# Sparse attention followed by a gated layer: where batch 1's attention sits inside batch 0's output products, and how batch 1's hidden layer begins

## The chip, the cores and the metric

The kernel runs on one core of a Trainium2 chip. That core has four compute engines, each with its own in-order stream of instructions: TensorE (PE in the profile; its weight loads are listed apart as PEld), VectorE (DVE), ScalarE (ACT) and GpSimd (POOL). A fifth stream, SyncE (SP), only issues DMA transfers; ACT and POOL issue some too. Streams wait for one another by semaphores, so an instruction that waits holds up everything behind it on its own engine.

The metric is the device time of one execution in microseconds (us). The kernel before was run three times: 217.37, 216.25 and 216.25, median 216.25.

## The reference, cut to what matters

Two stages. Attention over 4 batches, 8 heads, 768 positions and 64 channels a head: each query sees the keys less than 16 positions away, and one summary for each of the 24 blocks of 32 positions (largest key value per channel, mean of the values). Then a gated hidden layer over the 3072 rows of 512 channels.

```python
B, H, S, D = q.shape                       # 4, 8, 768, 64
block, window = (32, 16)
k_sum = k.reshape(B, H, nb, block, D).max(axis=3)
v_sum = v.reshape(B, H, nb, block, D).mean(axis=3)
scores_l = scale * np.matmul(q, k.transpose(0, 1, 3, 2))
mask_l = np.abs(pos[:, None] - pos[None, :]) < window
scores_s = scale * np.einsum('bhsd,bhnd->bhsn', q, k_sum) + np.log(block)
...                                        # softmax over both parts together
attn = np.matmul(a, np.concatenate([v, v_sum], axis=2))
x = attn.transpose(0, 2, 1, 3).reshape(B * S, H * D)
h = x @ w_in                               # 3072x512 by 512x2048
g = h * (1.0 / (1.0 + np.exp(-beta * h)))
out = g @ w_out                            # 3072x2048 by 2048x512
```

## The kernel before, in words

**Tiling.** Heads go in four pairs (g = 0..3), because two heads of 64 channels fill the 128 partitions. Batch by batch, three things are made:

- the attention output of the batch, laid down transposed in `xT` (four tiles of 128 channels by 768 rows; tile g comes from head pair g);
- the hidden layer `h_sb` (16 tiles of 128 hidden channels by 768 rows): for each tile, two halves of 384 rows, each a sum of four products over the four tiles of `xT` (L509), then one SiLU on ACT over both halves (L522);
- the output, six blocks of 128 rows, each a sum of 16 products of 128x512 (L527), copied from PSUM to SBUF and sent off by SP (L533). The sixteen products of a block are cut into four "atoms" of four, so there are 24 atoms in a batch.

**Staging.** The loops are software pipelined. While PE does the 24 output atoms of batch b, the attention of batch b+1 is put between the atoms; while it does the hidden layer of b+1, the inputs of batch b+2 are loaded, cast and transposed. The stage this study is about is the output of batch 0 with the attention of batch 1 in it, and the start of batch 1's hidden layer behind it.

**The order.** It is written out by hand. `run(main, sides)` walks through the main list (atoms 0 to 23), and after atom i gives out every side step whose position is below i + 1, in order of position. Each engine gets its instructions in the order in which the program gives them out. So a step at position 8.0 comes after atom 8, and its matmuls come before those of atom 9 on PE; the other engines' parts come in that order on their own streams.

**The steps of batch 1's attention**, for a head pair g and a half u of the rows:

- `load_v` (L103, L104) brings the values to `vst`; POOL casts them to `ve` (`v_cast`, L344); SP then moves rows of `ve` to `vo`, the copy shifted by half a tile, with two DMAs for each pair (`v_odd_dma`, L355 and L356). These are the "row moves" below.
- `km_pe` makes the largest key of each block on DVE (L233) and copies it beside the key windows on POOL (`key_sums`, L241).
- `scores` are 12 small matmuls (L328) into one of three PSUM buffers `big`, then an Exp on ACT (L335) and a multiplication by the band mask on DVE (`mask_e`, L339).
- `vm_all` makes the block means of the values for all four pairs, 28 matmuls (L388) into the PSUM buffer `one[1]`, and four DVE casts out of it; it needs all four `v_cast`s. `spread` writes these means into rows 96 to 127 of `vo` and `ve` on DVE (L399). Since the row moves read those rows of `ve`, the second half of `spread` (pairs 2 and 3) waits for the row moves of pairs 2 and 3.
- AV are 24 matmuls for each pair (L414) into `big`, then a reciprocal (L440) and a multiplication (L441) on DVE into `xn` (together "norm"). `x_dma` transposes `xn` into `xT[:, g]` by a DMA that ACT issues (L466).
- `key_load` (L97) brings the keys of the batch after next; it only shares SP's stream and the DMA engines with the steps above.

**Buffers.** `one` has two PSUM banks: atoms of an even output block use `one[0]`, of an odd one `one[1]`. `big` has three buffers of two banks, used in turn by scores, AV and the hidden tiles (tile i in `big[i % 3]`).

**Start of the hidden layer.** `h_tile(0)` does three quarters of tiles 0 and 1 (the products with pairs 0, 1 and 2) before the last quarter of tile 0, which needs pair 3. Inside `h_part` the order is half by half, so the third matmul of all already needs pair 2.

Of the kernel before, what the change touches and what calls it, by code (L numbers as in the profile page):

```python
# [11 lines left out]
def kernel(  # L12
# [10 lines left out]
    nc = tc.nc  # L23
# [27 lines left out]
    k1 = d_model // P  # L51
    k2 = d_ff // P
# [13 lines left out]
    one = [ps.tile([P, 1, 512], f32, name=f"one{i}") for i in range(2)]  # L66
# [3 lines left out]
    def pair(a, b, g):  # L70
        return a[b, 2 * g:2 * g + 2]
# [22 lines left out]
    def key_load(b, g):  # L94
        f = stage.tile([RK, 2, CK * D], f32, name="kst", tag="kst")
        stg[("k", b, g)] = f
        nc.sync.dma_start(out=f[:], in_=pair(k, b, g).rearrange("h (p c) d -> p h (c d)", c=CK))  # L97
# [186 lines left out]
    def km_pe(g, ks):  # L284
        key_max_win(g)
        key_sums(ks, g)
# [97 lines left out]
    def vm_all(t, cps):  # L384
        M = P - NK
        for j in range(J6 + 1):
            for g in range(G):
                nc.tensor.matmul(t[g * M:(g + 1) * M, 0, 0:2 * D], A[:, j],  # L388
                                 strided(ve[:, g, j, 0:1], [[J6 * VW, 2], [1, D]]),
                                 start=(j == 0), stop=(j == J6))  # L390
        for g in range(G):
            cps[g](vm_sb[NK:P, :, g], t[g * M:(g + 1) * M, 0, 0:2 * D].rearrange("p (h d) -> p h d", h=2))

    def spread(gg):
        r = slice(NK, P)
        s = slice(2 * gg, 2 * gg + 2)
        for tt in (vo, ve):
            for h in range(2):
                nc.vector.tensor_copy(out=tt[r, s, h * J6:(h + 1) * J6, 0:D],  # L399
                                      in_=vm_sb[r, h, s, None, :].to_broadcast([P - NK, 2, J6, D]))  # L400
# [64 lines left out]
    def x_dma(b, g):  # L465
        nc.scalar.dma_start_transpose(out=xT[:, g, :].rearrange("p (j t) -> p j t", j=J6),  # L466
                                    in_=xn[(b, g)].rearrange("p j h d -> p (j h d)"))
# [37 lines left out]
    def h_part(i, k_lo, k_hi):  # L505
        t = big[i % 3]
        for kk in range(2):
            for ki in range(k_lo, k_hi):
                nc.tensor.matmul(t[:, kk, 0:HS], w_in_sb[:, ki, i * P:(i + 1) * P],  # L509
                                 xT[:, ki, kk * HS:(kk + 1) * HS], start=(ki == 0), stop=(ki == k1 - 1))  # L510

    def h_tile(i):
        t = big[i % 3]
        if i > 1:
            h_part(i, 0, k1)
        elif i == 0:
            h_part(0, 0, k1 - 1)
            h_part(1, 0, k1 - 1)
            h_part(0, k1 - 1, k1)
        else:  # L520
            h_part(1, k1 - 1, k1)
        nc.scalar.activation(out=h_sb[:, i, :].rearrange("p (k m) -> p k m", k=2), in_=t[:, :, 0:HS],  # L522
                             func=ACTF.Silu, scale=beta_sb[:, i:i + 1])

# [27 lines left out]
    def run(main, sides):  # L552
        sides = sorted(sides, key=lambda x: x[0])
        for i, f in enumerate(main):
            f()
            while sides and sides[0][0] < i + 1:
                sides.pop(0)[1]()
        for _, f in sides:
            f()
# [83 lines left out]
    s = []  # L643
# [32 lines left out]
    s = [(6, lambda: scale4(1)), (12, lambda: scale4(2)), (.5, clear_kw), (14, lambda: km_pe(0, nc.gpsimd))]  # L676
# [4 lines left out]
    def av_at(b, s, pos, bufs):  # L681
        for g in range(G):
            def av(g=g):
                for u in range(2):
                    av_mm(b, g, u, big[bufs[g]][:, u])
                norm(b, g, big[bufs[g]], [0, 1])
                if g == 0 and b > 1:
                    for u in range(2):
                        last_mask[b] = mask_e(b, G - 1, u)
            s.append((pos[g], av))  # L690

    def x_pe2(b, g, t):
        t = t.bitcast(bf16)[:, 0, 0:S]
        x = xn[(b, g)]
        for j in range(J6):
# [1 line left out]
        act_cp(xT[:, g, :], t)  # L697

    s = [(.05, exp_table), (.15, lambda: scale4(3)), (.2, lambda: km_pe(1, nc.gpsimd)),
         (.3, lambda: km_pe(2, nc.gpsimd)), (3.44, lambda: km_pe(3, nc.gpsimd))]  # L700
    main = [lambda ms=ms, a=a: o_atom(0, ms, a) for ms in range(J6) for a in range(4)]
    s.append((2.5, lambda: qt1([act_cp, dve_cp])))
    for g in range(G):
        s.append(((2.88, 2.89, 3.4, 3.5)[g], lambda g=g: v_cast(nc.gpsimd, g)))
        s.append(((2.885, 2.895, 3.45, 3.55)[g], lambda g=g: v_odd_dma(g)))
    for j, (g, u, bg, pos, late) in enumerate([(0, 0, 2, 4.5, 4.6), (0, 1, 1, 4.5, 4.61), (1, 0, 0, 4.5, 4.62), (1, 1, 2, 8, 8.2),
                                               (2, 0, 1, 8, 8.21), (2, 1, 0, 8, 8.22), (3, 0, 2, 11, 11.13), (3, 1, 1, 11, 11.14)]):
        s.append((pos + .01 * j, lambda g=g, u=u, bg=bg: scores(1, g, u, bg)))
        s.append((late, lambda g=g, u=u: last_mask.update({1: mask_e(1, g, u)})))
    s.append((11.09, silu_table))  # L710
    s.append((8.0, lambda: vm_all(one[1], [dve_cp] * 4)))
    s.append((8.1, lambda: spread(0)))
    s.append((8.11, lambda: spread(1)))
    av_at(1, s, [11.12, 15.1, 15.2, 15.3], [0, 1, 2, 0])
    for g in range(G):
        s.append(((11.2, 15.35, 15.4, 15.5)[g], lambda g=g: x_dma(1, g)))
    for g in range(G):
        s.append(((2.896, 2.897, 3.56, 3.561)[g], lambda g=g: key_load(2, g)))
    run(main, s)


# [3 lines left out]
    for b in range(1, B):  # L725
        n = b + 1
        s = []
        if n < B:
            for g in range(2):
                s.append((0 + .1 * g, lambda g=g, n=n: hw_load("q", q, n, g)))  # L730
            for g in range(G):
                s.append((.5 + g, lambda g=g: key_cast(n, g)))
                s.append((.6 + g, lambda g=g: kq_dma("k", n, g)))
                s.append((3.5 + g, lambda g=g: windows_perm(dve_cp, g, kT[g][:, 0:S].rearrange("p (c r) -> p c r", c=CK), CK)))
                s.append((3.6 + g, lambda g=g: key_max_win(g)))
                s.append((4.7 + g, lambda g=g: kq_cast(nc.gpsimd, "q", n, g)))
                s.append((8 + g, lambda g=g: key_sums(nc.gpsimd, g)))
                s.append((6.6 + 1.5 * g, lambda g=g: kq_dma("q", n, g)))
                s.append((12.6 + 1.2 * g, lambda g=g: v_cast(nc.gpsimd, g)))
                s.append((12.7 + 1.2 * g, lambda g=g: v_odd_dma(g)))  # L740
            for g in range(2):
                s.append((.7 + g, lambda g=g, n=n: hw_load("q", q, n, g + 2)))
                s.append((2.7 + g, lambda g=g: load_v(n, g)))
                s.append((6.7 + 1.5 * g, lambda g=g: load_v(n, g + 2)))
        if n + 1 < B:
            for g in range(G):
                s.append(((16.31, 16.32, 19.3, 19.31)[g], lambda g=g, n=n: key_load(n + 1, g)))
        late = [x for x in s if x[0] >= 16]
        run([lambda i=i: h_tile(i) for i in range(k2)], [x for x in s if x[0] < 16])
        s = [((x[0] - 16) * 1.2, x[1]) for x in late]  # L750
        if n < B:
            for j, (g, u, bg, pos, late) in enumerate(UNITS):
                s.append((pos + .01 * j, lambda n=n, g=g, u=u, bg=bg: scores(n, g, u, bg)))
                if g < G - 1:
                    s.append((late, lambda n=n, g=g, u=u: mask_e(n, g, u)))
            s.append((.05, exp_table))
            s.append((11.19, silu_table))
            av_at(n, s, [11.2, 14.1, 14.2, 14.3], [0, 1, 2, 0])
            for g in range(G):
                s.append(((11.3, 14.35, 14.4, 14.5)[g], lambda g=g: x_dma(n, g)))  # L760
            s.append((5.89, lambda: vm_all(one[0], [dve_cp] * 4)))
            s.append((8.3, lambda: spread(0)))
            s.append((8.31, lambda: spread(1)))
        main = [lambda ms=ms, a=a: o_atom(b, ms, a) for ms in range(J6 - (n == B)) for a in range(4)]
        run(main, s)
        if n == B:
            ms = J6 - 1
            for lo, hi in ((0, 256), (256, 512)):
                t = one[0 if lo else 1][:, 0]
                for kk in range(k2):  # L770
                    o_mm(ms, kk, t, lo, hi)
                o = op.tile([P, hi - lo], f32, name="o_half", tag=f"o_half{lo}", bufs=1)
                nc.vector.tensor_copy(out=o[:], in_=t[:, 0:hi - lo])
                nc.sync.dma_start(out=out_r[b * J6 + ms][:, lo:hi], in_=o[:])
# [29 lines left out]
```

## Time and profile before

| | |
|---|---|
| median of the three runs | 216.25 us |
| the profiled execution | 216.76 us |
| its span (first to last instruction) | 214.9 us |
| PE busy | 205.3 us, 96% of the span |
| DVE busy | 111.0 us |
| ACT busy | 106.8 us |
| POOL busy | 54.6 us |
| hidden products L509 (batches 1 to 3) | 384 matmuls, 63.1 us |
| output products L527 | 83.4 us |
| granted TensorE clock | 0.998 of full speed |

The page's busy times are shares of the whole span. Where something starts and what it waited for is read from the timeline and from the chain that ended last; times in those are microseconds from the first instruction. In this execution batch 0's output atoms start at 48.40 us and batch 1's hidden layer at 77.37 us.

### The profile page before, as it was taken

To read this page: it belongs to the slowest core of one execution; us is meant where nothing else is said; L and a number is where in the kernel's file an instruction comes from. 1 tells how busy PE (TensorE), PEld (TensorE's weight loads), DVE (VectorE), ACT (ScalarE), POOL (GpSimd) and SP (SyncE) were. 2 spreads that over 40 slices of the span, in tenths; PEclk is the share of its full clock that TensorE was granted. 3 is DMA by queue.
4 is the path that set the end of the run, shared out by engine and by line. 5 is a ranking of instruction groups with operands and counts; after the bars stand their busy time and mean duration, and the time that the engine had idled before them with its cause. 6 is when DMAs were issued, how large, how long until landed. Compare 5 with 4: busy or idle time off the path is not lost.

```text
span 214.9 us, 5279 instructions
## 1 busy us (share of the span) xinstructions
PE 205.3 (96%) x2221; PEld 121.7 (57%) x2238; DVE 111.0 (52%) x252; ACT 106.8 (50%) x141; POOL 54.6 (25%) x85
## 2 busy tenths in 40 slices
PE   7999999999988999999999999999999999999993
PEld 7777766655454456665555466654555566654452
DVE  5587785398657721970898325654787200002121
ACT  2458786686655107778633046777450076650000
POOL 7938990003610303553103004443000000000000
PEclk9999999999999999999999999999999999999999
DMA  6999999999998999999689979999535500001212
GB/s 125 185 214 183 186 171 203 207 205 179 190 261 241 165 162 238 226 200 159 152 230 276 192 169 230 154 212 195 141 119 108 151 18 0 0 3 49 98 49 98
DMA packets 74534, 34.08 MB, mean 159 GB/s; under 512 B 61440, under 2 KB 70032, under 8 KB 74512
## 3 DMA queue, kind: packets, MB, share of 16 engines
q1 hardware_dynamic: 57440, 24.05, 53.2%
q0 software_dynamic: 7440, 7.34, 21.4%
q10 hardware_dynamic: 9632, 2.37, 8.0%
q8 instruction: 17, 0.28, 0.5%
q14 instruction: 5, 0.04, 0.1%
HBM read 27.37 MB, written 6.29 MB: 157 GB/s over the span
## 4 chain that ended last, share of the span: by engine, by line
PE 64%; DMA 15%; POOL 7%; DVE 6%; SPq 4%; issue 3%; ACT 0%; POOLq 0%; DVEq 0%
PE big L509 29%; PE one L527 29%; DMA w_out_sb<-in_moe_w_out_dram 8%; DMA xT<-xn 2%; DMA vst<-in_v_dram 2%; PE one L544 2%; DMA vo<-ve 2%; PE big L328 2%; PE big L414 2%; DVE xn L441 1%; SPq L356 1%; POOL ve L344 1%; POOL vo L351 1%; POOL vo L352 1%; DVE e L339 1%
## 5 line engine op out<-in xcount | busy, mean ns | idle before, releaser
L527 PE MATMUL one<-w_out_sb,h_sb 128*128 128x512 bf16 (+1 forms) x383 | 83.4, 370 | 1.9 <-issue 1.4
L522 ACT ACTIVATE h_sb<-big,beta_sb 128x768 bf16<-128x768 f32 x48 | 42.7, 900 | 47.1 <-PE big L509 47.1
L509 PE MATMUL big<-xT,w_in_sb 128*128 128x384 bf16 x384 | 63.1, 326 | 0.1
L527 PEld LDWEIGHTS <-h_sb 128*128 128x128 bf16 x400 | 38.1, 98 | 41.3 <-issue 0.2
L509 PEld LDWEIGHTS <-w_in_sb 128*128 128x128 bf16 x384 | 37.6, 98 | 25.5 <-issue 0.4
L247 DVE COPY o_sb<-one 128x512 f32<-128x512 f32 x19 | 13.1, 690 | 45.8 <-PE one L527 45.7
L335 ACT ACTIVATE e<-big,bias 128x768 bf16<-128x768 f32 x32 | 26.7, 897 | 15.8 <-PE big L328 13.7
L339 DVE TENSOR_TENSOR e<-e,mask 128x768 bf16<-128x768 bf16 x27 | 15.2, 584 | 13.9 <-ACT e L335 13.7
L247 DVE COPY kw<-kT 128x960 bf16<-128x960 bf16 (+1 forms) x16 | 10.6, 706 | 15.1 <-DMA kT<-kn 14.9
L344 POOL CAST ve<-vst 128x832 bf16<-128x832 f32 x15 | 13.6, 911 | 9.3 <-DMA vst<-in_v_dram 6.6
L475 POOL CAST qn<-qst 128x768 bf16<-128x768 f32 x8 | 6.6, 826 | 32.9 <-DMA qst<-in_q_dram 32.9
L241 POOL COPY kw<-km 128x288 bf16<-128x288 bf16 x12 | 7.8, 657 | 25.2 <-DVE km L233 25.2
L441 DVE TENSOR_TENSOR xn<-big,r 128x768 bf16<-128x768 f32 (+1 forms) x13 | 12.1, 927 | 0.4
L495 PE MATMUL big<-xT,w_in_sb 128*128 128x384 bf16 x64 | 11.6, 327 | 0.0
L233 DVE TENSOR_REDUCE km<-kw 128x24 bf16<-128x768 bf16 x12 | 11.3, 948 | 0.2
L641 ACT ACTIVATE h_sb<-big,beta_sb 128x384 bf16<-128x384 f32 x16 | 8.1, 579 | 3.1 <-PE big L495 3.1
L483 POOL CAST kn<-kst 96x1024 bf16<-96x1024 f32 x4 | 4.1, 1037 | 21.7 <-DVE e L339 21.6
L544 PE MATMUL one<-blank 128*128 128x128 bf16 (+1 forms) x105 | 7.9, 244 | 1.3 <-DVE blank L125 1.3
L501 PEld LDWEIGHTS <-w_in_sb 128*128 128x128 bf16 x64 | 6.2, 98 | 4.1
L501 PE MATMUL one<-xT,w_in_sb 128*128 128x384 bf16 x44 | 8.1, 326 | 0.0
L414 PEld LDWEIGHTS <-e 128*64 128x64 bf16 x336 | 6.2, 111 | 3.1 <-issue 1.9
L495 PEld LDWEIGHTS <-w_in_sb 128*128 128x128 bf16 x64 | 5.8, 98 | 3.4
(126 smaller groups left out, 188.8 us busy)
## 6 DMA issues: line engine op xcount, KB each, us to landing
out_dram<-o_sb SPq DMA_DIRECT2D x23, 256.0 KB, 2.5
vst<-in_v_dram SPq DMA_DIRECT2D x13, 336.0 KB, 4.8
kst<-in_k_dram SPq DMA_DIRECT2D x8, 384.0 KB, 5.6
qst<-in_q_dram SPq DMA_DIRECT2D x8, 384.0 KB, 4.2
w_in_sb<-in_moe_w_in_dram POOLq DMA_DIRECT2D x4, 512.0 KB, 5.6
w_out_sb<-in_moe_w_out_dram POOLq DMA_DIRECT2D x4, 512.0 KB, 14.2
vo<-ve SPq DMA_DIRECT2D x12, 107.2 KB, 3.1
vst<-in_v_dram SPq DMA_DIRECT2D x3, 416.0 KB, 6.9
```

What stands on the lines that cost most here:

```text
L233: nc.vector.tensor_reduce(out=km[g][:, NK:NK + nb].rearrange("p (m n) -> p m n", n=2), in_=kw[g][:, :, W:W + QT].rearrange("p m (n f) -> p ...
L247: nc.vector.tensor_copy(out=o, in_=i)
L335: return nc.scalar.activation(out=e[:], in_=s[:, :, 0:HS], func=ACTF.Exp, bias=bias[:, 0:1], scale=scale)
L339: return nc.vector.tensor_mul(out=e.rearrange("p h (m q) -> p h m q", q=QT), in0=e.rearrange("p h (m q) -> p h m q", q=QT), in1=mask[:, No ...
L344: eng.tensor_copy(out=ve[:, g, lo:hi, 0:D], in_=vst[g][:, lo:hi])
L441: nc.vector.tensor_mul(out=x[:, 3 * us[0]:3 * us[0] + 3 * n].rearrange("p (k j) h d -> p k (j h) d", k=n), in0=tv[:, :, :, 0:D], in1=r[:, ...
L495: nc.tensor.matmul(t[:, 0:HS], w_in_sb[:, ki, i * P:(i + 1) * P], xT[:, ki, 0:HS], start=(ki == 0), stop=(ki == k1 - 1))
L501: nc.tensor.matmul(t[:, 0:HS], w_in_sb[:, ki, i * P:(i + 1) * P], xT[:, ki, lo:lo + HS], start=(ki == 0), stop=(ki == k1 - 1))
L509: nc.tensor.matmul(t[:, kk, 0:HS], w_in_sb[:, ki, i * P:(i + 1) * P], xT[:, ki, kk * HS:(kk + 1) * HS], start=(ki == 0), stop=(ki == k1 - 1))
L522: nc.scalar.activation(out=h_sb[:, i, :].rearrange("p (k m) -> p k m", k=2), in_=t[:, :, 0:HS], func=ACTF.Silu, scale=beta_sb[:, i:i + 1])
L527: nc.tensor.matmul(t[:, 0:hi - lo], h_sb[:, n, ms * P:(ms + 1) * P], w_out_sb[:, n, lo:hi], start=(n == 0), stop=(n == k2 - 1))
L544: nc.tensor.matmul(t, blank[:, 0:P], blank[:, 0:t.shape[-1]], start=True, stop=True)
```

## The change

Four edits, all of them in how the work of batch 1 is ordered; the arithmetic is the same, and so is the number of instructions on the compute engines.

1. In the output stage of batch 0, the block sums (`vm_all`, `spread`), the scores of pairs 1 (second half), 2 and 3 with their masks, the table load for SiLU, AV of all pairs and their `x_dma` are put one atom later (8 becomes 9, 11 becomes 12, 15 becomes 16). The scores at 4.5 stay.
2. The loads of batch 2's keys: pairs 0 and 1 stood between the row moves of pairs 1 and 2; all four now stand behind the row moves of pair 3.
3. `km_pe(3)` goes from 3.44 to 3.52, which puts its POOL copy behind the cast of pair 3's values instead of ahead of it.
4. Batch 1's hidden layer begins on three tiles: the products of tiles 0, 1 and 2 with pairs 0 and 1 first (12 matmuls), then tiles 0 and 1 with pair 2 (4), then tile 0 with pair 3 (2), and then what is left of the three. Batches 2 and 3 keep the order that they had.

```diff
-    def h_tile(i):
+    BEGUN = {1: [[(0, 0, 2), (1, 0, 2), (2, 0, 2), (0, 2, 3), (1, 2, 3), (0, 3, 4)], [(2, 2, 3), (1, 3, 4)], [(2, 3, 4)]],
+             2: [[(0, 0, 3), (1, 0, 3), (0, 3, 4)], [(1, 3, 4)]]}
+    def h_tile(b, i):
         t = big[i % 3]
-        if i > 1:
-            h_part(i, 0, k1)
-        elif i == 0:
-            h_part(0, 0, k1 - 1)
-            h_part(1, 0, k1 - 1)
-            h_part(0, k1 - 1, k1)
-        else:
-            h_part(1, k1 - 1, k1)
+        begun = BEGUN[min(b, 2)]
+        for part in begun[i] if i < len(begun) else [(i, 0, k1)]:
+            h_part(*part)
...
-         (.3, lambda: km_pe(2, nc.gpsimd)), (3.44, lambda: km_pe(3, nc.gpsimd))]
+         (.3, lambda: km_pe(2, nc.gpsimd)), (3.52, lambda: km_pe(3, nc.gpsimd))]
...
-    for j, (g, u, bg, pos, late) in enumerate([(0, 0, 2, 4.5, 4.6), (0, 1, 1, 4.5, 4.61), (1, 0, 0, 4.5, 4.62), (1, 1, 2, 8, 8.2),
-                                               (2, 0, 1, 8, 8.21), (2, 1, 0, 8, 8.22), (3, 0, 2, 11, 11.13), (3, 1, 1, 11, 11.14)]):
+    for j, (g, u, bg, pos, late) in enumerate([(0, 0, 2, 4.5, 4.6), (0, 1, 1, 4.5, 4.61), (1, 0, 0, 4.5, 4.62), (1, 1, 2, 9, 9.2),
+                                               (2, 0, 1, 9, 9.21), (2, 1, 0, 9, 9.22), (3, 0, 2, 12, 12.13), (3, 1, 1, 12, 12.14)]):
...
-    s.append((11.09, silu_table))
-    s.append((8.0, lambda: vm_all(one[1], [dve_cp] * 4)))
-    s.append((8.1, lambda: spread(0)))
-    s.append((8.11, lambda: spread(1)))
-    av_at(1, s, [11.12, 15.1, 15.2, 15.3], [0, 1, 2, 0])
+    s.append((12.09, silu_table))
+    s.append((9.0, lambda: vm_all(one[1], [dve_cp] * 4)))
+    s.append((9.1, lambda: spread(0)))
+    s.append((9.11, lambda: spread(1)))
+    av_at(1, s, [12.12, 16.1, 16.2, 16.3], [0, 1, 2, 0])
     for g in range(G):
-        s.append(((11.2, 15.35, 15.4, 15.5)[g], lambda g=g: x_dma(1, g)))
+        s.append(((12.2, 16.35, 16.4, 16.5)[g], lambda g=g: x_dma(1, g)))
     for g in range(G):
-        s.append(((2.896, 2.897, 3.56, 3.561)[g], lambda g=g: key_load(2, g)))
+        s.append(((3.56, 3.561, 3.562, 3.563)[g], lambda g=g: key_load(2, g)))
```

In a triple such as `(2, 0, 2)` of `BEGUN` the first number is the hidden tile, and the other two bound the tiles of `xT` that are multiplied. Every row move, load and output of this stage goes through SP's stream; ACT issues the four transposes.

More of the change, by code (lines that the diff above doesn't have):

```diff
@@ L510, in h_part @@
                                  xT[:, ki, kk * HS:(kk + 1) * HS], start=(ki == 0), stop=(ki == k1 - 1))
-    def h_tile(i):
+    BEGUN = {1: [[(0, 0, 2), (1, 0, 2), (2, 0, 2), (0, 2, 3), (1, 2, 3), (0, 3, 4)], [(2, 2, 3), (1, 3, 4)], [(2, 3, 4)]],
+             2: [[(0, 0, 3), (1, 0, 3), (0, 3, 4)], [(1, 3, 4)]]}
+    assert k1 == 4
+    def h_tile(b, i):
         t = big[i % 3]
-        if i > 1:
-            h_part(i, 0, k1)
-        elif i == 0:
-            h_part(0, 0, k1 - 1)
-            h_part(1, 0, k1 - 1)
-            h_part(0, k1 - 1, k1)
-        else:
-            h_part(1, k1 - 1, k1)
+        begun = BEGUN[min(b, 2)]
+        for part in begun[i] if i < len(begun) else [(i, 0, k1)]:
+            h_part(*part)
         nc.scalar.activation(out=h_sb[:, i, :].rearrange("p (k m) -> p k m", k=2), in_=t[:, :, 0:HS],
@@ L748 @@
         late = [x for x in s if x[0] >= 16]
-        run([lambda i=i: h_tile(i) for i in range(k2)], [x for x in s if x[0] < 16])
+        run([lambda i=i: h_tile(b, i) for i in range(k2)], [x for x in s if x[0] < 16])
         s = [((x[0] - 16) * 1.2, x[1]) for x in late]
```

## The prediction

> **What bounds the kernel now.** I read the page's busy shares first, then the chain that ended last, then the waits between 50 and 80 us, then the timeline of that stretch. The page says that TensorE (PE) is the bound:
>
> ```profile
> PE 205.3 (96%) x2221; PEld 121.7 (57%) x2238; DVE 111.0 (52%) x252; ACT 106.8 (50%) x141; POOL 54.6 (25%) x85
> ```
>
> The chain tells where PE is not. Its columns are start, duration and what ran or was waited for.
>
> ```profile
> 58.49 0.58 SPq L97
> 59.12 0.45 SPq L97
> ...
> 59.67 0.40 SPq L533
> ...
> 61.53 4.09 DMA vo<-ve
> ...
> 65.75 0.63 DVE ve L399 x2
> ...
> 66.41 1.50 DVE e L339 x3
> ...
> 69.16 0.93 DVE e L339 x2
> ...
> 72.62 5.35 DMA xT<-xn
> 77.97 0.04 issue
> 78.01 20.64 PE big L509 x126
> ```
>
> From 78 us to the end the chain is nearly all PE: what is saved before 78 is saved at the end, as later loads hang on earlier steps of the same streams. Up to 78 it is a path of SP, DVE and DMAs: two key loads and an output go out ahead of pair 2's row move, the last `vo` move lands at 65.62, the second `spread` waits for it, masks and norms follow, and the transposes end it. The waits of that stretch (us in total, times, longest) name PE's losses:
>
> ```profile
> DVE ve L399 <- DMA vo<-ve: 2.3, 1, 2.3
> PE one L388 <- POOL ve L344: 0.8, 1, 0.8
> PEld L414 <- DVE e L339: 0.9, 2, 0.7
> PEld L509 <- issue: 0.4, 1, 0.4
> ```
>
> and the timeline has their places:
>
> ```profile
> 58.89 0.88 POOL L344 CAST ve<-vst 128x832 bf16<-128x832 f32 x1
> 59.82 0.56 PE L388 MATMUL one<-ve,A_avg 128*32 128x128 bf16 x25 [0.75 <-POOL ve L344]
> ```
>
> ```profile
> 70.68 6.85 PE L527 MATMUL one<-w_out_sb,h_sb 128*128 128x512 bf16 x31 [0.16 <-issue]
> 71.30 5.18 ACTq L466 DMA_TRANSPOSE xT<-xn  x3
> 77.37 6.80 PE L509 MATMUL big<-xT,w_in_sb 128*128 128x384 bf16 x39
> 80.16 2.53 ACT L522 ACTIVATE h_sb<-big,beta_sb 128x768 bf16<-128x768 f32 x3 [8.35 <-PE big L509]
> ```
>
> So PE stands for pair 3's value cast before the block sums, for pair 3's masks before its AV, and at 78.01 for pair 2's transpose.
>
> **Two rates.** Between 162.19 and 169.91 us the chain has 36 output matmuls without a wait (one record missing): 0.214 us each, so an atom is 0.857 us. A batch of 128 hidden matmuls takes 20.80 us there: 0.1625 us each.
>
> **Block sums an atom later.** They begin at 58.83; the matmul of pair 3 waits until 59.82, 0.05 after its cast ends at 59.77. With atom 9 ahead, PE works from about 58.74 to 59.60 and the same matmul starts at 59.82 again, with an atom more done. Gain 0.86. The scores behind it keep their time (60.31), and so do their Exps. The price: `one[1]` is needed again by atom 12, now two atoms behind the scores (about 62.9); the DVE casts out of it ended at 61.69.
>
> **`km_pe(3)` later.** On POOL the cast of pair 3 passes the 0.75 us key copy. The values of pair 3 landed at 53.96 + 4.8 = 58.76 (its DMA's time to landing), so the cast can't start before 58.8: gain 0, between 0 and 0.1. The copy then ends at about 60.3; who needs it, the scores of pair 3, starts at 63.6 or later. DVE's order does not change.
>
> **Key loads behind the row moves.** SP's stream is in order. After pair 1's second row move ends at 58.45, only the output (0.40) stands ahead of pair 2's moves; the two key loads (58.49 to 59.57) are gone. Pair 3's first move is issued at about 60.3 in place of 61.53; it needs the cast, 59.77. Its landing took 4.09 with 0.77 MB of key loads just ahead of it in the queue; the fastest row move here took 2.9. So it lands between 63.2 and 64.4, in place of 65.62. I take 64.4, the same row. DVE's stall of 2.3 shrinks to about 1.1: `spread` to 65.0, three masks to 66.6, norm of pair 0 to 67.8, the two masks of pair 3 to 68.8. Passed on SP: four key loads, about 0.55 each, go out from 61.5 to 63.7 rather than ending at 63.76, and the outputs behind them keep their time. POOL's casts of those keys waited for the mask until 70.16, so 1 to 3 us of later landing are covered; without that cover they would delay batch 2's keys, whose first use is 20 us away.
>
> **AV an atom later.** AV of pairs 1 and 2 starts at 68.15 as before, with an atom more done. Where nothing waits, 72 AV matmuls and the first output matmul behind them take 1.26 + 0.16 (chain, 160.77 to 162.19); here they took 70.68 - 68.15 = 2.53. Pair 3's AV then starts at 69.0; its masks are ready at 68.8 instead of 70.1. Gain 1.11; 0 if the row move lands as late as before. Seven atoms now cover norm and transposes, where it was eight.
>
> **Transposes and the start of h.** PE reaches h at 77.37 - 0.86 - 1.11 = 75.40. Norm of pair 1 started at 70.01, behind the masks; now AV of pair 1 releases it at about 68.65, 1.36 earlier, and norms 2 and 3 follow in the same 1.13 us steps. The three transposes were issued at 71.30, 72.62 and 74.5 and landed at 76.9, 77.97 and 79.1. Moved by 1.36: 75.54, 76.6, 77.7. In the new order the second matmul needs pair 1 (75.56), the thirteenth pair 2 (75.40 + 12 x 0.1625 = 77.35), the seventeenth pair 3 (78.0). All three just hold. In the order of before, pair 2 was due at the third matmul, and the stall was 78.01 - 77.37 - 2 x 0.1625 = 0.31. Gain 0.31. Bounds of the landing: batch 3's transposes took 2.7 to 3.6 where these took 4.6 to 5.6, so they may come up to 2 us earlier (no further gain); the slowest landing of the stretch is an output's 7.6 (issued at 64.5), with which pair 1 would come at 77.54 and cost 1.98. I take the 5.6 of the same transfer: 0.
>
> [...]
>
> **Three tiles begun.** The same 128 matmuls run, but SiLU of tile 0 now has only six matmuls (0.98) to hide behind before tile 3 needs its buffer, where it had ten. SiLU started 0.2 after the last matmul and takes 0.90: with 0.05 for the release, a stall of 0.15 (0 to 0.3). Later SiLUs step by 0.84 against 1.3 of PE a tile and are hidden.
>
> **Sum.** 0.86 + 0 + 1.11 + 0.31 - 0.15 = 2.1 us. The profiled execution took 216.76 (span 214.9), so it would take 214.7; it stood 0.5 above the median of 216.25, from which the sum gives 214.15. Leaning a little to the caution of transposes that only just hold, I say 214.3.
>
> **Rivals.**
>
> *A. The DVE path stays as it was.* If the last row move still lands at 65.62, masks and norms don't move: AV of pair 3 waits again and the transposes land as before. PE reaches h at 76.51, waits for pair 1 until 76.9 (0.23), and loses 0.15: gain 0.86 + 0.31 - 0.23 - 0.15 = 0.8, 215.5, within 0.5% (1.08 us, about what a measurement of this kernel can tell from no change). For it: the output and the values of pair 2 still share the queue. Against: SP's own wait disappears by the order of its stream. This is also the case in which putting the key loads later does nothing.
>
> *B. A tenth of the cover.* The path gets shorter, but the transposes land 0.4 to 1.0 later than forecast, as pair 0's overlaps the draining key loads: 214.7 to 215.15; at the middle 214.9. For it: 0 slack at pair 1, 0.3 at pair 3. Against: between 62 and 69 us the queue of SP moved about 0.28 MB a us, so 1.57 MB of keys and the outputs with them are through at about 70, when pair 1's transpose starts.
>
> *C. Slower: the key loads hold the transposes up.* Place: ACT's DMA queue from 67 to 78 us. h starts in effect at pair 1's landing less 0.16, plus 0.15 for SiLU; before, at 78.01 - 0.325 = 77.69. So it decides at pair 1 landing at 77.7, 2.1 later than forecast and 0.8 later than before. A landing of 9 us gives 78.9: 1.2 slower, 217.5. Against: only an output took as long as 7.6, and no transpose did. [...]
>
> **Chances.** Forecast 0.66 (its own range 213.8 to 214.7), B 0.12, A 0.15, C 0.07. Faster by over 0.5% are forecast and B, 0.78; within 0.5% is A, 0.15; slower is C, 0.07. The range starts at 213.8 (no SiLU stall, and the cast 0.1 earlier) and reaches past A to 215.7; C and the ends of the forecast's own range are left out.
>
> **What the changed profile would show.** Right: the 0.75 before L388 gone, with vm_all still at 59.8; SP's L97 as one group of four behind the last L356; DVE's wait for the row move near 1 us or less; AV of pairs 1 to 3 in one run of 1.26 at 68.1 to 69.4; h's first matmul at 75.4 and no gap up to the eighteenth; a gap of 0.1 to 0.2 before tile 3; and the rest shifted by 2 us. Wrong: a row move that still lands past 65 (A), or a wait of h for a transpose (B, C).

## The result and the profile after

The changed kernel took 214.68 us in the median of 22 executions, beside 215.82 for 22 of the kernel before. The ratio is 0.9952, with a 95% interval from 0.9934 to 0.9971: faster by 0.48%, about 1.0 us. This interval leaves out no change; that of a later comparison, on another chip, just includes it: 0.9975 (0.9949 to 1.0002). The profiled execution took 215.10 with a span of 213.2. Two of the profiles below, of the variants keys_only and no_keys, come from slow executions (219.42 and 217.56 us), while the ratios of these variants come from their other executions.

The page of the kernel after, part 1 and the chain by engine:

```profile
PE 205.9 (97%) x2238; PEld 120.9 (57%) x2238; DVE 109.9 (52%) x252; ACT 106.8 (50%) x141; POOL 53.8 (25%) x85
...
PE 91%; DMA 3%; DVE 2%; POOL 1%; issue 1%; POOLq 0%; DVEq 0%
```

The chain was 64% PE in the first profile of the kernel before and is 91% PE here. The whole share is no measure of the change, as the stretch ahead of this stage counts in it too: the kernel before, profiled again, has 84%. What matters is this stage. SP has left the chain there, and from the scores at 55.23 on DMAs and DVE have too: up to the end of the hidden layer it is PE alone. The same chain in order of time (start, duration, what):

```profile
55.93 4.42 PE one L526 x20
60.35 0.51 PE one L388 x26
...
68.70 1.26 PE big L414 x72
69.96 6.15 PE one L526 x28
76.11 3.90 PE big L509 x24
80.01 0.01 issue
80.03 17.06 PE big L509 x104
```

The block sums take 0.51 and the AV of three pairs 1.26, both without a wait. What is left is a gap before the 25th hidden matmul, ahead of tile 3: the last three pieces end at 97.09, 20.98 after 76.11, where 128 hidden matmuls without a wait take 20.80. The timeline has the other engines:

```profile
58.88 0.88 POOL L344 CAST ve<-vst 128x832 bf16<-128x832 f32 x1 [1.46 <-DMA vst<-in_v_dram]
60.83 0.60 SPq L356 DMA_DIRECT2D vo<-ve  x1
61.47 2.08 SPq L97 DMA_DIRECT2D kst<-in_k_dram  x4
63.87 0.62 DVE L399 COPY ve<-vm_sb 32x768 bf16<-32x768 bf16 x2
69.27 0.23 DVE L440 RECIPROCAL r<-big 128x12 f32<-128x12 f32 x1 [1.06 <-PE big L414]
70.53 5.11 ACTq L466 DMA_TRANSPOSE xT<-xn  x3
75.95 8.30 PE L509 MATMUL big<-xT,w_in_sb 128*128 128x384 bf16 x49
79.07 3.35 ACT L521 ACTIVATE h_sb<-big,beta_sb 128x768 bf16<-128x768 f32 x4 [9.76 <-PE big L509]
```

The four key loads stand behind the last row move, the second `spread` (63.87) has no wait in front of it, and now DVE waits for PE (1.06 before pair 1's norm) instead of the other way round.

So the steps all happened. In these two executions the stage gains what the sum said: from the first output atom to the first hidden matmul it took 28.97 before (48.40 to 77.37) and 26.97 after (48.98 to 75.95); with 0.31 of wait for a transpose before and 0.18 ahead of tile 3 after, the gain is 2.13, where 2.1 was predicted. The two execution times differ by less, 216.76 - 215.10 = 1.66, because the output atoms of the second started 0.58 later. But the medians differ by about half of 2.13. The rest of this text is about where the other half is.

### The profile page after: what moved, and what is told of

It reads as the page before. It is cut to its first block, busy times and chain, and to the rows that moved or that the text cites. A ratio compares the mean times of both kernels' runs of the same rounds, so it can differ in the third digit from the quotient of the medians.

```text
span 213.2 us, 5296 instructions
## 1 busy us (share of the span) xinstructions
PE 205.9 (97%) x2238; PEld 120.9 (57%) x2238; DVE 109.9 (52%) x252; ACT 106.8 (50%) x141; POOL 53.8 (25%) x85
## 4 chain that ended last, share of the span: by engine, by line
PE 91%; DMA 3%; DVE 2%; POOL 1%; issue 1%; POOLq 0%; DVEq 0%
PE one L526 39%; PE big L509 29%; PE big L495 5%; PE one L501 3%; DMA qrow<-in_q_dram 3%; PE big L414 2%; PE big L328 2%; DVE qn L247 2%; PE big L501 2%; PE big L276 1%; PE big L315 1%; PE big L307 1%; PE one L388 1%; POOL krow L87 1%; PE big L260 1%
## 5 line engine op out<-in xcount | busy, mean ns | idle before, releaser
L526 PE MATMUL one<-w_out_sb,h_sb 128*128 128x512 bf16 (+1 forms) x400 | 85.8, 371 | 0.0
L241 POOL COPY kw<-km 128x288 bf16<-128x288 bf16 x12 | 6.9, 581 | 25.6 <-DVE km L233 25.6
L543 PE MATMUL one<-blank 128*128 128x128 bf16 (+1 forms) x105 | 7.4, 235 | 1.3 <-DVE blank L125 1.3
L503 ACT ACTIVATE h_sb<-one,beta_sb 128x384 bf16<-128x384 f32 x11 | 6.4, 582 | 2.2 <-PE one L501 1.7
```

Of the source, the lines that this page charges most:

```text
L526: nc.tensor.matmul(t[:, 0:hi - lo], h_sb[:, n, ms * P:(ms + 1) * P], w_out_sb[:, n, lo:hi], start=(n == 0), stop=(n == k2 - 1))
```

## The experiments

Two theories were put against each other. S: the waits of the first profiled execution are typical of the kernel, and half of the gain is lost somewhere. V: the waits differ from execution to execution, and that one had more than usual.

The wait ahead of the block sums is read as the time from the first matmul of the atoms ahead of them to the scores behind them, less 4.93 with the atom more (the changed kernel's time, which has no wait), or less 4.07 without it. The wait ahead of pair 3's AV is the time between the output blocks on both sides of AV, less 4.82, the same in all executions without a wait. In the first profile:

```profile
55.27 3.63 PE L527 MATMUL one<-w_out_sb,h_sb 128*128 128x512 bf16 x15
...
60.31 0.70 PE L328 MATMUL big<-qn,kw 64*128 64x64 bf16 x36
...
64.81 3.40 PE L527 MATMUL one<-w_out_sb,h_sb 128*128 128x512 bf16 x15 [0.16 <-issue]
```

So the first wait is 60.31 - 55.27 - 4.07 = 0.97. The block behind AV began at 70.68, and the second wait is 70.68 - 64.81 - 4.82 = 1.05.

**The kernel before, two more times.** No edit.

> The kernel before once more, for a second profiled execution. Theory S (the waits of the profiled execution are typical): the output atoms start near 48.4 us, PE again waits about 0.75 before the block sums, 1.1 before pair 3's AV and 0.3 at the third hidden matmul, and the profiled time is near 216.7. Theory V (the waits differ from execution to execution, because the DMA path to the row moves doesn't start with PE's own path): with another start of the atoms or another landing of the last row move the three waits add up to something else, between 0.5 and 1.7 us where the first profile had 2.2, and the profiled time is lower than 216.7 by about the difference. Timed: same as before, within 0.3%.

> The kernel before a third time. Theory V: PE's waits ahead of the block sums and ahead of pair 3's AV again differ from the first profile's 0.97 and 1.05 (the second profile had 0.30 and 0.51), with a sum between 0.8 and 2.0 us, and the profiled time goes with that sum and with the start of the output atoms. Theory S: 0.9 and 1.1 again.

Measured: ratios 0.9998 (0.9972 to 1.0024) and 1.0018 (0.9987 to 1.005), as it should be for the same kernel. The profiled executions took 214.97 and 215.31 us, where the first took 216.76. The waits of the first of them, and its timeline on PE and DVE:

```profile
DVE ve L399 <- DMA vo<-ve: 1.8, 1, 1.8
...
PEld L414 <- DVE e L339: 0.4, 2, 0.2
```

```profile
55.22 3.63 PE L527 MATMUL one<-w_out_sb,h_sb 128*128 128x512 bf16 x16
...
58.78 0.88 PE L388 MATMUL one<-ve,A_avg 128*32 128x128 bf16 x28
59.59 0.70 PE L328 MATMUL big<-qn,kw 64*128 64x64 bf16 x36
...
63.87 3.63 PE L527 MATMUL one<-w_out_sb,h_sb 128*128 128x512 bf16 x16
69.20 7.08 PE L527 MATMUL one<-w_out_sb,h_sb 128*128 128x512 bf16 x32
76.12 2.11 PE L509 MATMUL big<-xT,w_in_sb 128*128 128x384 bf16 x12
```

The 0.75 ahead of L388's last pair is not in the list any more (the sums take 0.81 rather than 0.51, and 59.59 - 55.22 - 4.07 = 0.30), AV waits 69.20 - 63.87 - 4.82 = 0.51 instead of 1.05, and the hidden layer starts without a wait. The sum of the waits ahead of the block sums, of AV and at the third hidden matmul is 0.81 here, 0.94 in the third profile and 2.33 in the first. Theory S falls: the waits are not a property of the kernel alone, and the prediction was made from the execution with the most of the three. In the first profile SP began to issue batch 1's values at 47.20, 1.2 ahead of the first output atom; in the other two at 45.74 and 46.18, 2.6 and 2.1 ahead of it.

**One edit alone.**

```diff
# begin_only: batch 1's hidden layer on three tiles, nothing else
...
+    BEGUN = {1: [[(0, 0, 2), (1, 0, 2), (2, 0, 2), (0, 2, 3), (1, 2, 3), (0, 3, 4)], [(2, 2, 3), (1, 3, 4)], [(2, 3, 4)]],
...
```

> Only the beginning of batch 1's hidden layer on three tiles. Theory S: the wait of 0.31 at the third matmul goes, as pair 2 is due only at the thirteenth, and 0.15 to 0.2 come in before tile 3: faster by 0.15 us, no change that can be measured. Theory V: the same terms, smaller gain, 0 to 0.15 us slower where an execution has no wait for pair 2. In the trace: a gap of about 0.17 after 24 hidden matmuls in either case.

Measured: 1.0001 (0.9973 to 1.0028), no change, as both theories had it. Its profile shows the gap of 0.18 ahead of tile 3, and another division of the waits: 1.37 ahead of the block sums, 0.07 ahead of AV.

```diff
# keys_only: key loads behind the row moves, key copy behind the cast
-         (.3, lambda: km_pe(2, nc.gpsimd)), (3.44, lambda: km_pe(3, nc.gpsimd))]
+         (.3, lambda: km_pe(2, nc.gpsimd)), (3.52, lambda: km_pe(3, nc.gpsimd))]
-        s.append(((2.896, 2.897, 3.56, 3.561)[g], lambda g=g: key_load(2, g)))
+        s.append(((3.56, 3.561, 3.562, 3.563)[g], lambda g=g: key_load(2, g)))
```

> Only the key loads behind the row moves (with the key copy behind pair 3's cast). Theory S: the last row move lands 1.2 to 2.4 us earlier, pair 3's masks are ready before PE comes to its AV, the transposes land 1.3 earlier; the wait before the block sums stays at 0.75: faster by 1.1 + 0.3 = 1.4 us (0.65%). Theory V: the same waits go, but they are about half as long in a usual execution: faster by 0.5 to 0.9 us (0.2 to 0.4%). If the transposes suffer from the later key loads (rival C of the prediction), slower.

Measured: 0.9958 (0.9936 to 0.998), faster by 0.42%, 0.9 us: theory V's upper end, while S's 1.4 us lies just outside the interval. In its profile AV had no wait (68.47 - 63.65 is 4.82). That execution is the one that took 219.42; what else happened in it is told under the hardware.

```diff
# atom_only: block sums, later scores, AV and transposes an atom later
-    av_at(1, s, [11.12, 15.1, 15.2, 15.3], [0, 1, 2, 0])
+    av_at(1, s, [12.12, 16.1, 16.2, 16.3], [0, 1, 2, 0])
...
```

> Only the block sums, later scores, AV and transposes an atom later; keys and hidden layer as before. Theory S: the wait before the block sums goes (0.86), but the masks of pair 3 and the transposes keep their times, so PE only comes to the same waits earlier: the wait at the third hidden matmul grows from 0.31 to about 1.2, and the whole is within 0.1 us of before. Theory V: the same, with 0 to 0.4 us faster in executions where the transposes are not the last to land.

Measured: 0.9969 (0.994 to 0.9997), faster by 0.31%, 0.7 us. Theory S said no change within 0.1 us and theory V 0 to 0.4 us; the measured gain is above both, and its interval, from 0.1 to 1.3 us, just reaches S and holds most of V, so time does not part them. Its profile has the block sums without a wait, 0.39 ahead of AV and 0.26 at the third hidden matmul: PE does come to the other waits sooner, but they are small.

**One edit left out of the changed kernel.**

```diff
# no_keys: key loads and key copy where they were
...
+        s.append(((2.896, 2.897, 3.56, 3.561)[g], lambda g=g: key_load(2, g)))
# no_atom: the old atoms
...
+    av_at(1, s, [11.12, 15.1, 15.2, 15.3], [0, 1, 2, 0])
# no_begin: the old start of the hidden layer
...
+            h_part(0, 0, k1 - 1)
...
```

> The changed kernel with the key loads and the key copy where they were (an atom later and three tiles begun). Theory S (the waits of the first profiled execution are typical): PE comes 0.86 earlier, the DVE path keeps its times, so 0.8 us faster than before (0.37%). Theory V (the waits differ between executions: in the other profiled executions of before's order the one ahead of the block sums was 0.3 and 1.4, the one ahead of pair 3's AV 0.5 and 0.1): the wait of the block sums goes, most of the other stays, 0.15 goes to the SiLU ahead of tile 3: faster by 0.3 to 0.7 us. In the trace: DVE's wait for the row move stays at 1.3 to 2.3 us.

> The changed kernel with block sums, later scores, AV and transposes at their old atoms (key loads behind the row moves, three tiles begun). Theory S: 1.11 + 0.31 - 0.15 = 1.27 us faster than before (0.6%), and PE still waits 0.75 to 0.97 for the cast ahead of the block sums. Theory V: the wait ahead of the block sums is anything from 0.1 to 1.4, that of AV is gone: faster by 0.4 to 1.0 us.

> The changed kernel with the hidden layer begun as before (two tiles, pair 2 due at the third matmul). Theory S: PE comes to the hidden layer at 75.4, pair 2 lands at 76.6, so 0.9 is waited there and 0.15 of SiLU is saved: 1.4 us faster than before and 0.7 slower than the changed kernel. Theory V, from the changed kernel's own profile (first hidden matmul at 75.95, pair 1 landed at 75.6, pair 2 at 76.3, pair 3 at 77.6): the wait is 0.1 to 0.4 and 0.17 is saved, so as fast as the changed kernel within 0.2 us: 0.9 to 1.2 us faster than before.

Measured: 0.9982 (0.9959 to 1.0006), 0.997 (0.9945 to 0.9996) and 0.9986 (0.9954 to 1.0019), with medians of 214.77, 214.97 and 215.0 us. The three can't be told apart by time. Their profiles can: no_keys keeps 0.51 ahead of AV and DVE's wait for the row move of 1.7; no_atom keeps 1.39 ahead of the block sums and none ahead of AV; no_begin has neither, and waits 0.26 for pair 2's transpose at the third hidden matmul. Each edit takes away the wait that it was said to. In time, no_atom (0.6 us faster) fits V's 0.4 to 1.0 and not S's 1.27; no_keys (0.4) fits V's 0.3 to 0.7, but its interval holds S's 0.8 too; the interval of no_begin reaches from 1.0 us faster to 0.4 slower, which holds no change and V's 0.9, and not S's 1.4.

**SiLU ahead of tile 3.**

```diff
# tile0_first and tile0_again, on the changed kernel
-    BEGUN = {1: [[(0, 0, 2), (1, 0, 2), (2, 0, 2), (0, 2, 3), (1, 2, 3), (0, 3, 4)], [(2, 2, 3), (1, 3, 4)], [(2, 3, 4)]],
+    BEGUN = {1: [[(0, 0, 2), (1, 0, 2), (2, 0, 2), (0, 2, 4)], [(1, 2, 4)], [(2, 2, 4)]],
```

> The changed kernel with both last quarters of tile 0 ahead of those of tile 1 (12 matmuls with pairs 0 and 1, then four of tile 0, four of tile 1, four of tile 2). If the 0.17 us that PE loses ahead of tile 3 is the SiLU of tile 0, which has six matmuls (0.98) to hide behind: with eight (1.3) the gap is gone, 0.15 to 0.17 us less than the changed kernel, as long as pair 3 (due at the 15th matmul, 2.3 after the first) has landed. If the gap is something else (a buffer's release by DVE, a weight load), it stays at 24 matmuls or moves by its own cause. In time: 1.1 to 1.4 us faster than before.

> The changed kernel once more, beside the next one. Theory V: 0.9 to 1.4 us faster than before (0.4 to 0.65%), with a smaller spread of the times than before has, as the waits that differ between executions are gone; 0 to 0.3 us of wait between the first output atom and the hidden layer, 0.17 ahead of tile 3. Theory S: 2.1 us faster (1%).

> The changed kernel with both last quarters of tile 0 first, a second time and next to the changed kernel: 0.1 to 0.2 us less than it, as the 0.17 ahead of tile 3 is gone, which is below what these rounds can tell; in the trace no gap in the 128 hidden matmuls (20.80 us).

Measured: tile0_first 0.9962 (0.9941 to 0.9984) of before; later, on another chip, after_again 0.9975 (0.9949 to 1.0002) and tile0_again 0.9966 (0.9938 to 0.9994), with medians of 214.58 and 214.66. In the chain of tile0_again the hidden layer is one piece:

```profile
75.42 20.80 PE big L509 x128
```

The gap of 0.18 is gone, so it was SiLU's, and eight matmuls cover it. The two profiled executions of this order are the fastest two of all that were profiled (214.39 and 214.36). In time the 0.18 is below what these ratios can tell: this order beats the kernel before, and it is not shown to beat the changed one.

**The values let go sooner.**

```diff
# before_v2, on the kernel before
-                behind(i, wo[3])
+                behind(i, wo[2])
```

> The kernel before, with batch 1's value loads let go one transfer sooner (behind the third quarter of w_out in place of the fourth). From 25 to 52 us the DMA engines are full, so the values come earlier only at the cost of what was ahead of them. If the waits ahead of the block sums and AV are set by when the values come: they shrink to 0 to 0.3 and 0 to 0.3, and DVE's wait for the row move stays (the key loads still stand there). The queries of batch 1, which land just in time at 51 (PE waited 0.4 for them), may come later and give back 0.3 to 1.0. In time: between 0.5 us faster and 0.3 slower than before. If the waits stay as they are although the values land earlier, the cause is not the values' landing.

Measured: 1.0032 (1.0002 to 1.0062), slower by 0.3%, 0.7 us, where at most 0.3 us was expected. SP issues the first values at 43.74 instead of 45.74 to 47.20, but those of the last pair at 52.99, where the three profiles of before have 53.53, 52.56 and 52.95, and the queries come later:

```profile
PEld L276 <- DMA qrow<-in_q_dram: 0.7, 1, 0.7
...
PE big L276 <- DMA qrow<-in_q_dram: 0.2, 1, 0.2
```

The queries cost PE the 0.2 of the second line in this execution; the rest of the 0.7 is not accounted for. The wait ahead of the block sums is 0.30 and that of AV 0.45, as in the other two profiles. So letting the first values go sooner did not bring the last of them sooner, and the run does not test what an earlier landing would do. In the first profile of before the DMA engines' mean busy share, in stretches of 3 and 6 us, is 1.07 to 1.25 all the way from 25 to 52 us, which fits, but is not shown to be the cause.

The profiles do show what goes with the wait ahead of the block sums. It is not the moment of the first values: no_atom issued them at 46.09, 2.2 ahead of the first output atom, and has the largest wait. It is the moment of the last pair's. In the five profiles with the old atom that the table below holds they were issued 4.2, 4.6, 5.1, 5.4 and 5.4 after the first output atom, and the waits are 0.30, 0.58, 0.97, 1.37 and 1.39. Why that moment differs between executions stays open.

**The profiles together**, without before_v2 and the two named at the start. Waits in us; "start" is the first output atom; the last column is the profiled time less start and waits.

| kernel | start | sums | AV | transpose | tile 3 | time | rest |
|---|---|---|---|---|---|---|---|
| before, first | 48.40 | 0.97 | 1.05 | 0.31 | 0 | 216.76 | 166.0 |
| before_again | 48.34 | 0.30 | 0.51 | 0 | 0 | 214.97 | 165.8 |
| before_third | 48.32 | 0.58 | 0.36 | 0 | 0 | 215.31 | 166.1 |
| begin_only | 48.25 | 1.37 | 0.07 | 0 | 0.18 | 215.93 | 166.1 |
| atom_only | 49.52 | 0 | 0.39 | 0.26 | 0 | 215.95 | 165.8 |
| no_atom | 48.27 | 1.39 | 0 | 0 | 0.18 | 215.76 | 165.9 |
| no_begin | 48.65 | 0 | 0 | 0.26 | 0 | 215.06 | 166.2 |
| after | 48.98 | 0 | 0 | 0 | 0.18 | 215.10 | 165.9 |
| after_again | 48.51 | 0 | 0 | 0 | 0.18 | 214.64 | 165.9 |
| tile0_first | 48.23 | 0 | 0 | 0 | 0 | 214.39 | 166.2 |
| tile0_again | 48.30 | 0 | 0 | 0 | 0 | 214.36 | 166.1 |

The rest is 166.0 within 0.2 us for every order. Nothing is given back later: what an execution takes is its start, 166.0, and its waits. That holds for no_keys too, whose 217.56 is mostly a late start: 50.85, with waits of 0.51 and 0.18, leaves 166.0. The three profiles of before have waits of 2.33, 0.81 and 0.94, 1.36 in the mean; less the 0.18 that comes in ahead of tile 3, the gain is 1.2 us in the mean of three, and the timed ratio says 1.0 (0.6 to 1.4).

## Why the prediction was right in its direction and too large in its size

*The bound, and nothing lost after 78 us:* right. The chain is PE from 55.23 to the end of the hidden layer, and the rest is the same in all orders.

*Block sums an atom later, gain 0.86:* right in what it does; the wait is gone in every profile that has the edit. The size was near the middle: 0.97, 0.30, 0.58, 1.37 and 1.39 in the five profiles of the table with the old atom, 0.92 in the mean.

*Key copy later, gain 0:* the cast of pair 3 started at 58.88, still waiting for its values, as predicted from the first profile. In before_again it was otherwise: the last values landed at 57.6 (issued at 52.99, 4.6 to landing), and the cast began at 57.85, as the key copy ended (57.16 + 0.74). There the copy held it up by about 0.25 us, more than the prediction's "between 0 and 0.1". *Key loads behind the row moves:* the mechanism was right, and the landing too cautious. The last first-half row move landed 2.1 us after issue, at 62.4, where 4.1 and 64.4 were taken, so DVE's wait did not shrink to 1.1 but went. (The row move at 65.62 that the prediction calls the last is the last that `spread` waits for; its second half landed 0.3 later.) *Transposes:* pair 1 was issued at 70.53 and landed 5.1 later, at 75.6; it was due at 76.1, and the others had room too. Taking the 5.6 of the same transfer was right.

*AV an atom later, gain 1.11:* this is the term that was mis-sized. The wait that it takes away was 1.05 in the execution that the prediction was made from; it was 0.51, 0.36, 0.07 and 0.39 in the four others of the table with the old key loads. It also isn't independent of the first wait: where the cast was latest (1.37), PE came to AV so much later that 0.07 was left there. *The third hidden matmul, gain 0.31:* 0.31 in the first profile and 0 in the other two of before.

*Three tiles begun, cost 0.15:* right, 0.18. Where pair 2 is late it pays (0.26 was waited without it in no_begin); by time alone it could not be shown to do either.

*The sum:* 2.1 is what the stage gained between the two profiled executions. The step that failed is the one that took the sum off the median instead of off the execution that it was read from. The waits that were added up are what made that execution slow: it stood 0.5 above the median of three, and 0.9 above the 215.82 of 22. The prediction gave both readings, 214.7 for the profiled execution less the sum and 214.15 for the median less the sum, and leaned to the second with 214.3. The measured median is 214.68. What is left when varying waits are taken out is a floor. From whichever execution one starts it is the same, but for the start of the output atoms, which differs too (48.23 to 49.52 in the table). That 214.3, between the two readings, lies only 0.4 from the measured median owes something to luck: the sum was about twice the measured gain, and it was taken off a median of three, 216.25, that stood 0.4 above the one of 22.

*The rivals:* A (the DVE path stays) is no_keys: its waits of 0.51 ahead of AV and 1.7 for the row move are there, at 0.2% faster. B, transposes that land late, was not needed. C was not the usual case: in the changed kernel's profile the transposes landed after 5.1, 4.4 and 4.4, no later than before. One execution of keys_only, below, looks like C; that the key loads held its transposes up is not shown. On the chances: 0.78 stood on faster by over 0.5%, and the 0.48% that was measured is just on the other side of that line.

## What to carry to other kernels

A wait that depends on when a DMA lands can differ from execution to execution; here the same kernel had 2.33, 0.81 and 0.94 us of such waits. Before a sum of waits is taken off, compare the profiled execution with the median, or profile the kernel again: the sum belongs to that execution, and time less sum is the floor, as far as the stage starts at the usual time. And two waits on one path are not independent: what the first holds up, the second may no longer have to (1.37 and 0.07 in begin_only).

## What the runs showed of the hardware that was not expected

*With the key loads behind them the row moves landed in about half the time.* In the profile of the changed kernel the row moves of pairs 2 and 3 landed in 2.0 to 2.1 us, with one output of 256 KB ahead of them in SP's stream. Behind two key loads of 384 KB and one output the same moves took 3.9 to 4.8 in the first profile of before. For pair 3's first move, the one DVE waits for, it is 2.1 beside 3.5 to 4.1 in the three profiles of before; the prediction allowed 2.9 to 4.1.

*After two stops of PE its granted clock was down.* In the profiled execution of keys_only the first transpose was issued at 65.9, while SP's queue was still moving data (94% to 108% of the 16 DMA engines' time in the half microseconds from 67 to 68.5 us), and landed 8.9 us later; the one that PE then waited for took 7.5. It looks like rival C, in one execution of the seven profiled with late key loads. That the key loads held the transposes up is not shown: an output issued behind them, at 62.78, took 8.4 us to landing, and from 70 to 72 us the DMA engines moved only 40 GB/s, where they moved 183 in the changed kernel's profile. What followed PE's stop can be read. These are stretches of time (length, PE busy, PEld, DVE, ACT and POOL busy with instructions, granted clock, DMA share, GB/s):

```profile
76.00:78.00 2.00, 0.00 (x0) 0.00 (x0) 0.87 (x2) 0.00 (x0) 0.00 (x0) 1.00 0.46 138
...
79.20:79.70 0.50, 0.50 (x5) 0.29 (x3) 0.00 (x0) 0.00 (x0) 0.00 (x0) 0.74 1.27 290
79.70:80.20 0.50, 0.50 (x3) 0.20 (x2) 0.00 (x0) 0.00 (x0) 0.00 (x0) 0.50 1.37 227
...
82.50:83.00 0.50, 0.50 (x3) 0.26 (x2) 0.00 (x0) 0.50 (x2) 0.00 (x0) 0.65 1.34 216
83.00:83.50 0.50, 0.50 (x5) 0.30 (x4) 0.00 (x0) 0.50 (x1) 0.29 (x1) 1.00 1.25 278
```

PE stood from about 75.9 to 78.72. The granted clock was still 1.00 when it went on, fell to 0.50 between 79.2 and 79.7, and was back at 83. The 126 hidden matmuls from there took 22.32 us rather than 20.64, so 1.7 was lost on top of the wait of 2.8.

The profiled execution of no_keys shows the same thing a second time, near its beginning. PE waited for the first queries, and then:

```profile
PE big L260 <- DMA qrow<-in_q_dram: 1.8, 1, 1.8
...
12.00:14.00 2.00, 2.00 (x31) 1.74 (x32) 0.75 (x2) 0.80 (x1) 0.33 (x1) 0.63 0.70 143
14.00:16.00 2.00, 2.00 (x34) 1.46 (x33) 0.83 (x1) 0.00 (x0) 0.62 (x2) 0.51 1.25 252
```

PE stood for 1.8 us until 11.96, and the clock was down from about 12.5 to 16. Its output atoms started at 50.85, where the table has 48.23 to 49.52. In the changed kernel's profile PE stood for 1.37 us at the same place and the clock stayed at 1.00. So of the stops seen here those of 1.8 and 2.8 us were followed by half the clock, and the one of 1.37 was not.
